# First modulations in three steps, and the first block's FFN1 as one stretch of 64-row products

## The chip, the cores and the metric

One core of a Trainium2 chip runs the whole program. The metric is the device time of one execution in microseconds (us), the median of several runs. The engines are PE (TensorE, matrix products and transposes), DVE (VectorE), ACT (ScalarE), POOL (GpSimd) and SP (SyncE, which here only issues DMAs). A product of PE reads a stationary operand that was loaded before (LDWEIGHTS, shown as PEld) and streams the other through it; it writes to PSUM, from which DVE or ACT take the result.

## What is computed

A transformer block whose normalised inputs and branches are modulated by a vector c. x is 2048 tokens by 576, all data are bf16.

```python
mod = (silu(c) @ w_mod).reshape(1, 6, 1, 576)
sa, ca, ga, sb, cb, gb = mod[:, 0] ... mod[:, 5]
h = layernorm(x) * (1 + ca) + sa
x = x + ga * attention(h)          # wqkv, feature maps, wo
h = layernorm(x) * (1 + cb) + sb
x = x + gb * (relu(h @ w1) @ w2)   # 576 -> 4608 -> 576
```

The attention is linear: 32 heads of 18, each q and k goes through a matrix w_phi of its head, and the feature map is softmax(p) beside softmax(-p).

```python
phi_q = concat([softmax(pq), softmax(-pq)]); phi_k = likewise
kv = einsum('bhsf,bhsd->bhfd', phi_k, v);  z = phi_k summed over tokens
o  = einsum('bhqf,bhfd->bhqd', phi_q, kv) / (einsum('bhqf,bhf->bhq', phi_q, z) + 1e-6)
```

## The kernel before

The 2048 tokens are 16 tiles of 128, and for the second half eight blocks of two tiles. 576 features are five chunks of rows: four of 128 and one of 64, "the half chunk" (chunk 4).

**Start.** w_mod's first 1152 columns (sa and ca, "the first modulations") are loaded into wma: one DMA for chunks 0 to 3 and one for the half chunk (load_first_mods, step LH; load_rows). first_mods(r), step MC1.r, multiplies silu(c) with them: 25 products of one column each, r = 1 the scale (ca) and r = 0 the shift (sa). first_scale (MSC) adds 1 to the scale and puts it in SBUF; first_shift (MSH) casts the shift. wqkv's columns, folded with w_phi on the chip, are multiplied by the scale into wv_sb and wfold (fold_scale, steps SCv and SC1), and the shift gives a bias row (fold_bias, steps Bv and B1, tile ps_bias). PT transposes the first normalised tiles on PE (psT_h). After that every projection (steps K, V, Q; ps_k, ps_v, ps_q) can run.

**Attention.** For each pair of tiles the feature maps take a maximum by a tree of halvings (MN, qMN), two subtractions (HI, LO; qHI, qLO) on DVE, exps on ACT (EX, qEX), row sums on DVE or PE (SU, qSD), a logarithm and an exp on ACT that give the reciprocal (RC, qRC) and a scaling on DVE (SC, qSC). Steps with a q belong to the queries of later tiles. qT transposes the map of a pair of tiles by DMA into ET. The sums kv over all tokens stand in ps_kv (KVa to KVc) and are copied with a mask into KVZ (KVE, line 640 on ACT or 642 on DVE). Then NU, NV multiply ET with KVZ (ps_num, ps_nun; NU for tiles 0 and 1, NV for 2 and 3), NUE and NVE divide (rq, o_tm), OT and OU transpose the result into oT, WO and WP multiply by wo (wo_mm for the first tiles of block 1; ps_wo), WOE and WPE add to the residual x_sb. The aux pool that holds ps_wo has two buffers, one tile of ps_wo for each half of the 576 columns; the pool of ps_h has three.

**FFN.** Per block and q = 0 to 8, FFN1 makes 4 × 128 rows of the hidden layer for 256 tokens in one PSUM tile ps_h, RL.q applies relu on ACT into H; FFN2 (step Y, ffn2_step, tile ps_y) reads H and w_sb. A step Y.j.h.p is a third (p) of the products of tile j and column half h, so it needs the relus of q = 3p to 3p + 2. In the first block FFN1 is written with G.g and FW.q: f1_whole is 16 products of 128 rows per q, f1_pairs 4 products of 64 rows per q for the half chunk, one for each half of the output partitions' set e; three q share one run of half-chunk products. In blocks 1 to 3 and after them FFN1 and wo are written in 64-row products throughout (f1_rows, wo_rows, row_halves): phase 0 multiplies rows 0 to 63 into output half e = 0 and rows 64 to 127 into e = 1, in turn, phase 1 the other way. Phase 1 must not begin in a bank before phase 0 has ended there, so a POOL memset (tile token, line 838) waits for phase 0's last product and phase 1's first product waits for it. ffn1_rows puts phase 0 of the next q between the two.

```python
for hh in range(2):
    for ci in ((4, 0, 1, 2, 3) if phase == 0 else (0, 1, 2, 3)):
        for r in range(2):
            s, e = slice(r * 64, r * 64 + 64), r ^ phase
            items.append((f1[q][:, e, hh * w:hh * w + w], l, hT[s, ci, :]))
```

**What sets the order.** Up to the end of the first block's FFN2 the program order is one string, order, at lines 1021 to 1044: names of steps (explained in the dictionary above it), in which each step issues its instructions in turn; an engine executes its own in that order. Blocks 1 to 7 are in block(n): tables say behind which product group a piece of another block's work is issued. A DMA of SP or ACT takes one of eight semaphores in turn and waits for the DMA eight before it. SP's weight loads are steps LW (w1a, w1b, w1c) and W2 (w_sb); RD.1 loads row_gb. PN transposes tiles 0 and 1 after the second norm (psT_n) and PNE modulates them into hT2all, which FFN1 reads; MCE2 adds 1 to the second scale.

Of the kernel before, what the change touches and what calls it, by code (L numbers as in the profile page):

```python
# [8 lines left out]
P = 128  # L9
# [34 lines left out]
def kernel(  # L44
# [115 lines left out]
    def load_first_mods():  # L160
        load_rows(nc.sync, wma, w_mod, 0, 2 * D)
# [44 lines left out]

# [100 lines left out]
    def first_mods(r):  # L307

        mod_ps[1, r] = aux_tile("ps_mod")
        for ci in range(KC):  # L310
            for ck in range(KC):
                o = (ck * 2 + r) * D + ci * P
                T_.matmul(mod_ps[1, r][:, ci:ci + 1], lhsT=wma_[:, o:o + P], rhs=siluc[:, ck, :],
                          start=(ck == 0), stop=(ck == KC - 1))
# [400 lines left out]
    def wo_pair(n, j):  # L715

        onum["wo", n, j] = [aux_tile("ps_wo") for _ in HALVES]
        for i, (p, (cs, cn)) in enumerate(zip(onum["wo", n, j], HALVES)):
            r = slice(i * 64, i * 64 + 64)
            T_.matmul(p[:, 0:cn], lhsT=oTs[n, j][r, 4, :], rhs=wo_sb[r, 4, cs:cs + cn], start=True, stop=False)  # L720

    def wo_mm(n, j):
        ps = onum.get(("wo", n, j))
        if ps is None:
            ps = onum["wo", n, j] = [aux_tile("ps_wo") for _ in HALVES]
            proj(ps, oTs[n, j], wo_sb, HALVES)
        else:
            for p, (cs, cn) in zip(ps, HALVES):
                for ci in range(4):
                    T_.matmul(p[:, 0:cn], lhsT=oTs[n, j][:, ci, :], rhs=wo_sb[:, ci, cs:cs + cn], start=False, stop=(ci == 3))  # L730
# [81 lines left out]
    def f1_pairs(n, q, first):  # L812
        hT, w = hT2[n], U * P
        for hh in range(2):
            for e in range(2):
                r = slice(e * 64, e * 64 + 64)
                T_.matmul(f1[q][:, e, hh * w:hh * w + w], lhsT=w1["c"][r, 2 * q + hh, :], rhs=hT[r, 4, :],  # L817
                          start=(first and hh == 0), stop=(not first and hh == 1))

    def f1_whole(n, q, first):  # L820
        hT, w = hT2[n], U * P
        for ci in range(4):
            for hh in range(2):
                for e in range(2):
                    T_.matmul(f1[q][:, e, hh * w:hh * w + w], lhsT=w1_at(2 * q + hh, e, ci),  # L825
                              rhs=hT[:, ci, :], start=(first and hh == 0 and ci == 0),
                              stop=(not first and hh == 1 and ci == 3))
# [92 lines left out]
    def ffn1(n, qs, behind={}):  # L920

        f1_open(n, qs)
        for i, q in enumerate(qs):
            f1_whole(n, q, i == 0)
            if i == 0:
                first = behind.get((q, "pairs"))
                if first:
                    first()
                for k, p in enumerate(qs):
                    f1_pairs(n, p, k > 0)  # L930
                if (q, "half") in behind:
                    behind[q, "half"]()
            f1_relu(q)
            if q in behind:
                behind[q]()

    def f1_group(g):
        qs = (3 * g, 3 * g + 1, 3 * g + 2)
        f1_open(0, qs)
        f1_whole(0, qs[0], True)  # L940
        for k, p in enumerate(qs):
            f1_pairs(0, p, k > 0)
# [28 lines left out]
    def y(n, j, cols=HALVES):  # L971
# [59 lines left out]
    QE.1 LT.11 Q.7 KE.8.1 MX.1 EX.0 QE.7 LS.15 Q.0 LX.6 Q.3 LO.3 QE.0 RS.7 SU.0 K.10 LT.9 QE.3.1 HI.3 K.11 K.9 EX.1
    KE.11 LO.2 WOL qMN.0 SA.0 LX.7 KE.10 KE.9 LT.12 SU.1 HI.2 EX.3 K.12 RW.1 RW.0 MN.2 SA.1 qMX.0 KE.12 LT.15 SU.3
    RWE.0.1 LT.14 K.15 RC.0 W1 qLO.0 K.14 RWE.1.1 LO.4 EX.2 KE.15 qHI.0 LT.13 Q.14 LO.5 MX.2 SA.3 KE.14 qEX.0 QE.14
    K.13 V.9 RC.1 HI.5 SU.2 HI.4 RC2.0 KE.13 MN.3 Q.4 LW.1.1 LO.7 VE.9 qEX.1 SA.2 V.8 EX.4 EX.5 QE.4.1 Q.13 MX.3 V.6
    VE.8 LO.6 SC.0 qSU.0 V.13 RC.2 SC.2 VE.6 qSA.0 RD.2 QE.13 Q.12 SU.5 RC.3 HI.6 VE.13 SC.3 qRC.0 V.10 EX.6 SU.4 VE.10
    SA.5 RC2.2 V.11 RC.5 QE.12 VE.11 qSC.0 V.12 SA.4 HI.7 EX.7 SC.1 SD.12 Q.8 V.15 RD.0 SD.13 SC.5 VE.12 VE.15 SU.7
    RC.4 SA.7 SC.4 RC.6 V.14 qT.0 QE.8 KVa LW.1.0 SC.6 VE.14 RC.7 KVb RC2.1 SC.7 LW.0.0 KVc Q.11 WS.1 KVE.0 KVE.1.1
    LW.0.1 QE.11 NU.1 Q.6 NU.0 LW.2.0 WS.0 NUE.1 OT.1 QE.6 Q.10 NUE.0 OT.0 OTE.1 WO.1 OTE.0 qMN.1 QE.10.1 WOE.1 WO.0
    Q.5 S2.1.1 Q.9 WOE.0 Q.15 R2.1 S2.0 R2.0 X2.1 qLO.1 X2.0 PN.1 P2 MCE2 QE.9 PN.0 QE.5.1 W2.1.1 LW.3.1 W2.0.0 PNE
# [137 lines left out]
```

## Time and profile before

| | us |
|---|---|
| median of 3 runs | 410.82 |
| the three runs | 410.12 to 411.81 |
| the profiled execution, own time | 410.89 |
| its span, first to last instruction | 409.1 |
| PE busy | 401.2 |
| DVE busy | 232.7 |
| ACT busy | 181.3 |
| granted TensorE clock | 1.000 |

The profile comes from one execution. Its span lies 1.8 us under that execution's time. PE's time is the busy time of its instructions, DVE's and ACT's likewise; a share near 100% says that the engine is the bound unless its instructions are themselves slow. The chain that ended last is followed back from the last instruction to the first: each row of it is a stretch in which that one thing held up the end, with start, length, engine, tile, line and the number of instructions. The timeline names in square brackets the idle time before an instruction and what ended it. In the table of DMA issues the last number is the median time from issue to landing.

The whole of the first block's FFN1 stands between 101.71 and 120.19 us, its FFN2 ends at 140.99, and block 1's FFN1 begins there.

### The profile page before, as it was taken

Reading aid. Unit: us, or ns where it says so; the run is one execution under the profiler, and the core shown is the slowest. Engines: PE = TensorE matmul, PEld = TensorE weight load, DVE = VectorE, ACT = ScalarE, POOL = GpSimd, SP = SyncE. Lnnn points to the kernel's source line nnn. Section 1 sums busy time; section 2 is a strip of 40 time slices with the busy share of each in tenths; the row PEclk is TensorE's granted clock in tenths of the full one; section 3 lists DMA queues with packets and bytes.
Section 4 is the critical chain, followed back from the end, with each engine's and each line's share of the span. In section 5 each row is a group of like instructions: output and inputs, shape, how many; then the busy total and the mean of one; then the engine's idle time right before and its main releaser. Section 6 shows DMA issues by size and latency. Waiting matters only on the chain.

```text
span 409.1 us, 10340 instructions
## 1 busy us (share of the span) xinstructions
PE 401.2 (98%) x4416; PEld 299.3 (73%) x4416; DVE 232.7 (57%) x600; ACT 181.3 (44%) x339; POOL 18.2 (4%) x112
## 2 busy tenths in 40 slices
PE   6999999999999999999999999999999999999997
PEld 3777777787887888888888888654467774447776
DVE  5889999999838586976886579523202310000121
ACT  5799999945761065216421460144530005552000
POOL 8100000000000000000000000000000000000000
DMA  8967950499861541424273216500040000000000
GB/s 254 281 102 200 217 126 18 73 248 375 272 159 32 118 48 23 101 48 72 54 99 80 42 34 86 112 2 2 2 66 14 16 23 8 2 2 0 16 16 29
DMA packets 70983, 35.50 MB, mean 87 GB/s; under 512 B 56657, under 2 KB 67418, under 8 KB 70938
## 3 DMA queue, kind: packets, MB, share of 16 engines
q1 hardware_dynamic: 70336, 34.83, 36.9%
q8 instruction: 34, 0.56, 0.6%
q10 hardware_dynamic: 602, 0.02, 0.1%
q14 instruction: 11, 0.09, 0.1%
HBM read 19.27 MB, written 2.37 MB: 53 GB/s over the span
## 4 chain that ended last, share of the span: by engine, by line
PE 95%; DMA 3%; DVE 0%; ACT 0%; SPq 0%; issue 0%
PE ps_y L957 35%; PE ps_h L834 30%; PE ps_v L449 5%; PE ps_k L449 5%; PE ps_q L449 5%; PE ps_h L825 4%; PE ps_wo L834 3%; PE ps_sum L515 2%; DMA wma<-in_w_mod_dram 2%; PE ps_kv L628 1%; PE ps_wo L449 1%; DMA kv_raw<-in_A_wqkv_dram 1%; PE ps_num L669 1%; PE ps_h L817 1%; PE ps_bias L366 1%; PE ps_fold L345 0%
## 5 line engine op out<-in xcount | busy, mean ns | idle before, releaser
L957 PE MATMUL ps_y<-w_sb,H 128*128 128x288 bf16 x864 | 109.0, 286 | 0.0
L957 PEld LDWEIGHTS <-H 128*128 128x128 bf16 x864 | 83.2, 98 | 22.0 <-issue 1.5
L965 DVE TENSOR_TENSOR outt<-ps_y,row_gb 128x288 bf16<-128x288 f32 (+2 forms) x33 | 14.7, 446 | 101.3 <-PE ps_y L957 101.3
L834 PE MATMUL ps_h<-hT2all,w1a 64*128 64x256 bf16 (+1 forms) x800 | 68.6, 312 | 0.0
L890 ACT ACTIVATE H<-ps_h 128x512 bf16<-128x512 f32 x36 | 21.5, 596 | 81.3 <-PE ps_h L834 81.3
L449 PEld LDWEIGHTS <-hT 128*128 128x128 bf16 x480 | 45.9, 97 | 12.6 <-issue 0.5
L834 PE MATMUL ps_h<-hT2all,w1b 64*128 64x256 bf16 (+1 forms) x640 | 54.9, 312 | 0.0
L834 PEld LDWEIGHTS <-w1a 64*128 64x128 bf16 x800 | 38.9, 94 | 21.1
L917 ACT ACTIVATE H<-ps_h 128x1024 bf16<-128x1024 f32 x36 | 36.1, 1018 | 35.3 <-PE ps_h L834 31.8
L834 PEld LDWEIGHTS <-w1b 64*128 64x128 bf16 x640 | 31.2, 94 | 17.3
L735 DVE TENSOR_TENSOR x_sb<-x_sb,ps_wo 128x288 bf16<-128x288 bf16 x28 | 11.6, 450 | 38.8 <-PE ps_wo L834 37.5
L957 PE MATMUL ps_y<-w_sb,H1m 128*128 128x288 bf16 (+2 forms) x270 | 32.4, 273 | 0.0
L834 PE MATMUL ps_h<-hT2all,w1c 64*128 64x256 bf16 (+1 forms) x180 | 28.4, 313 | 0.0
L957 PEld LDWEIGHTS <-H1m 128*128 128x128 bf16 x270 | 24.5, 98 | 5.2
L508 ACT ACTIVATE room<-room 128x1188 bf16<-128x1188 bf16 x16 | 18.7, 1189 | 15.9 <-DVE room L481 15.9
L449 PE MATMUL ps_v<-wv_sb,hT 128*128 128x288 bf16 x160 | 21.6, 286 | 0.0
L449 PE MATMUL ps_q<-wfold,hT 128*128 128x270 bf16 (+1 forms) x160 | 21.4, 285 | 0.0
L449 PE MATMUL ps_k<-wfold,hT 128*128 128x270 bf16 (+1 forms) x160 | 21.4, 285 | 0.0
L838 POOL MEMSET token<- 1x2 bf16 x75 | 7.1, 94 | 314.1 <-PE ps_h L834 298.2
L226 DVE BATCH_NORM_STATS2 bst<-x_sb 128x6 f32<-128x288 bf16 x46 | 18.5, 444 | 1.1 <-DMA x_sb<-in_A_x_dram 1.1
L526 DVE TENSOR_REDUCE ln_s<-room 128x66 f32<-128x1188 bf16 x14 | 18.9, 1373 | 0.1
L891 ACT ACTIVATE H1m<-ps_h 128x512 bf16<-128x512 f32 x30 | 17.8, 592 | 0.0
(165 smaller groups left out, 476.5 us busy)
## 6 DMA issues: line engine op xcount, KB each, us to landing
w_sb<-in_B_w_dram SPq DMA_DIRECT2D x6, 864.0 KB, 7.5
out_dram<-outt SPq DMA_DIRECT2D x15, 144.0 KB, 1.8
w1b<-in_B_w_dram SPq DMA_DIRECT2D x2, 1024.0 KB, 9.6
x_sb<-in_A_x_dram SPq DMA_DIRECT2D x3, 576.0 KB, 7.3
w1a<-in_B_w_dram SPq DMA_DIRECT2D x2, 768.0 KB, 4.6
kv_raw<-in_A_wqkv_dram SPq DMA_DIRECT2D x4, 288.0 KB, 5.0
wma<-in_w_mod_dram SPq DMA_DIRECT2D x1, 1152.0 KB
wmb<-in_w_mod_dram SPq DMA_DIRECT2D x2, 576.0 KB, 4.3
```

Of the source, the lines that this page charges most:

```text
L226: V.bn_stats(out=st[:, half, :], in_=x_sb[:, t0 + j, half * 288:(half + 1) * 288])
L449: T_.matmul(ps[:, 0:cn], lhsT=lhs[:, ci, :], rhs=w[:, ci, cs:cs + cn], start=(ci == 0), stop=(ci == KC - 1))
L508: A_.activation(out=E[:, j:j + k], in_=E[:, j:j + k], func=ACT.Exp)
L526: V.tensor_reduce(out=t["l", b][:, k * 22:(k + 1) * 22].rearrange("p (g s) h -> p g s h", s=2), op=ALU.add, axis=mybir.AxisListType.X, in_ ...
L735: V.tensor_tensor(out=xs[:, cs:cs + cn], in0=xs[:, cs:cs + cn], in1=p[:, 0:cn], op=ALU.add)
L825: T_.matmul(f1[q][:, e, hh * w:hh * w + w], lhsT=w1_at(2 * q + hh, e, ci), rhs=hT[:, ci, :], start=(first and hh == 0 and ci == 0), stop=( ...
L834: i = T_.matmul(ps, lhsT=l, rhs=r, start=(phase == 0 and k < 2), stop=(phase == 1 and k >= len(items) - 2))
L890: A_.activation(out=p2t["H1"].rearrange("p (e j) n -> p e j n", e=2)[:, :, i, :], in_=f1[i][:, :, 0:U * P], func=ACT.Relu)
L891: A_.activation(out=h1_more(i), in_=f1[i][:, :, U * P:], func=ACT.Relu)
L917: A_.activation(out=p2t["H1"].rearrange("p (e j) n -> p e j n", e=2)[:, :, 2 * q:2 * q + 2], in_=f1[q][:].rearrange("p e (h n) -> p e h n" ...
L957: T_.matmul(ps[:, 0, 0:cn], lhsT=h, rhs=p2t["w2"][:, k, c], start=(k == 0), stop=(k == NJ - 1))
L965: V.tensor_tensor(out=o[:, c], in0=ps[:, 0, 0:cn], in1=rows["gb"][:, c], op=ALU.mult)
```

## The change

Three things are edited, and a new order string goes with them.

1. load_first_mods brings the half chunk (64 rows, 144 KB) first, then chunks 0 and 1 and chunks 2 and 3, 576 KB each, in place of chunks 0 to 3 in one load and the half chunk last. first_mods runs in three steps: MC1.0 takes chunks 4, 0 and 1 of scale and shift without one product, 29 in all; MC1.1 the 11 that the scale still lacks; MC1.2 the 10 of the shift. The transposes PT.0 now stand between MC1.0 and MC1.1.
2. The first block's FFN1 goes through f1_rows (steps HA.q and HB.q for the two phases) and wo of tiles 2 and 3 through wo_rows (WA, WB). wo_pair, wo_mm, f1_pairs, f1_whole, ffn1 and f1_group are removed. The attention steps of tiles 4 and 5 (NW, NWE, OW, as att(2, 0) and att(2, 1) before) move from block 1's FFN1 into the first block's FFN2; block 1's table is rewritten accordingly.
3. The order string is new where this needs it, and around 88 to 102 us: KVE.1 on DVE instead of ACT, MCE2 earlier, the copies QE.10 and QE.5 on ACT, Q.5 behind PN and PNE, qHI.2 and qLO.2 behind the first NVE.0, the weight loads in another order.

```diff
     def load_first_mods():
-        load_rows(nc.sync, wma, w_mod, 0, 2 * D)
+        nc.sync.dma_start(wma[0:64, 4, :], w_mod[512:576, 0:2 * D])
+        for k in (0, 2):
+            nc.sync.dma_start(wma[:, k:k + 2, :], w_mod[k * P:(k + 2) * P, 0:2 * D].rearrange("(k p) n -> p k n", p=P))
...
     def first_mods(r):
-        mod_ps[1, r] = aux_tile("ps_mod")
-        for ci in range(KC):
-            for ck in range(KC):
-                o = (ck * 2 + r) * D + ci * P
-                T_.matmul(mod_ps[1, r][:, ci:ci + 1], lhsT=wma_[:, o:o + P], rhs=siluc[:, ck, :],
-                          start=(ck == 0), stop=(ck == KC - 1))
+        if not r:
+            mod_ps[1, 1], mod_ps[1, 0] = aux_tile("ps_mod"), aux_tile("ps_mod")
+        late = [(1, 1, KC - 1)] + [(1, ck, ci) for ck in (2, 3) for ci in range(KC)]
+        if r == 0:
+            todo = [(s, ck, ci) for s in (1, 0) for ck in (4, 0, 1) for ci in range(KC) if (s, ck, ci) not in late]
+        else:
+            todo = late if r == 1 else [(0, ck, ci) for ck in (2, 3) for ci in range(KC)]
+        for s, ck, ci in todo:
+            o = (ck * 2 + s) * D + ci * P
+            T_.matmul(mod_ps[1, s][:, ci:ci + 1], lhsT=wma_[:, o:o + P], rhs=siluc[:, ck, :],
+                      start=(ck == 4 and ci == 0), stop=(ck == 3 and ci == KC - 1))
...
-        "P2": open_p2, "G": f1_group, "FW": lambda q: f1_whole(0, q, False), "RL": f1_relu,
+        "P2": open_p2, "HA": lambda q: f1_rows(0, q, 0), "HB": lambda q: f1_rows(0, q, 1), "RL": f1_relu,
...
+        "NW": lambda j: num(2, j), "NWE": lambda j: quotient(2, j), "OW": lambda j: o_T(2, j),
-        "WP": lambda j: wo_mm(1, j), "WPE": lambda j: wo_out(1, j), "S3": lambda j: ln3[1](j),
+        "WA": lambda j: wo_rows(1, j, 0), "WB": lambda j: wo_rows(1, j, 1), "WPE": lambda j: wo_out(1, j), "S3": lambda j: ln3[1](j),
...
-    qMX.1 QE.15 qHI.1 qMX.2 G.0 LW.3.0 qMN.2 qLO.2 qEX.2 LW.2.1 FW.2 qEX.3 FW.1 RL.2 W2.1.0 RD.1 qHI.2 RL.0 RL.1 qSD.3
-    G.1 W2.0.1 RL.3 qSD.2 FW.4 qRC.1 W2.2.0 qSC.1 RL.4 FW.5 qT.1 RL.5 G.2 qEX.5 FW.8 FW.7 NV.0 NVE.0 RL.8 qEX.4 RL.7
+    HA.0 HA.1 HA.2 qMN.2 HB.0 LW.2.0 P2 HB.1 qSD.3 qEX.2 HB.2 qSD.2 LW.3.1 qMX.2 LW.3.0 W2.0.0 W2.1.0 RL.0 W2.0.1 HA.3
+    RL.1 qRC.1 RL.2 RD.1 HA.4 HB.3 HB.4 HA.5 RL.3 HA.6 W2.2.1 HB.5 RL.5 qSC.1 HB.6 W2.1.1 qT.1 NV.0 RL.6 Y.1.0.0 NVE.0
+    W2.2.0 OU.0 NV.1 qHI.2 RL.4 Y.1.0.1 HA.7 qLO.2 NVE.1 qEX.4 qSD.4 qEX.5 HA.8 OU.1 WA.0 HB.7 WB.0 qSD.5 WPE.0 qRC.2
+    HB.8 RL.7 WA.1 Y.1.1.0 qSC.2 WB.1 Y.1.1.1 WPE.1 RL.8 Y.1.0.2 S3.0 S3.1 Y.0.0.0 R3 X3 Y.1.1.2 YE.1.0 qT.2 NW.0 XT
...
         if n == 1:
-            F(3, "low")()
-            F(3, "high")()
-            ffn1_rows(n, {("b", 0): [att(2, 0)], ("b", 2): [att(2, 1), F(3, "exps", 0)], ("b", 3): [F(3, "exps", 1)],
...
-            normed(2)()
-            turned(2)()
+            ffn1_rows(n, {("a", 0): [F(3, "low"), F(3, "high")], ("b", 1): [early(2, 0)], ("b", 2): [late(2, 0), F(3, "exps", 0)],
+                          ("b", 3): [F(3, "exps", 1)], ("b", 4): [early(2, 1), F(3, "sums", 0)],
+                          ("b", 5): [late(2, 1), F(3, "sums", 1), normed(2), turned(2)], ("b", 6): [F(3, "recip", 0)],
+                          ("b", 7): [F(3, "scale", 0), turn(3)]})
```

Three places show how the instructions move. SP issues the FFN's weight loads just ahead of the transposes ET of tiles 2 and 3 (row_gb is the row of the second gate). Before:

```order
L767 DMA w1c<-in_B_w_dram 64x2304 x2
L772 DMA w1a<-in_B_w_dram 128x4x512
L778 DMA w_sb<-in_B_w_dram 128x6x576
L774 DMA w1b<-in_B_w_dram 128x4x1024
L778 DMA w_sb<-in_B_w_dram 128x6x576
L774 DMA w1b<-in_B_w_dram 128x4x1024
L772 DMA w1a<-in_B_w_dram 128x4x512
L778 DMA w_sb<-in_B_w_dram 128x6x576
L410 DMA row_gb<-four_d 128x576
L778 DMA w_sb<-in_B_w_dram 128x6x576 x2
L656 DMA_TRANSPOSE ET<-room 128x11x128 x2
L778 DMA w_sb<-in_B_w_dram 128x6x576
```

and with the change:

```order
L757 DMA w1c<-in_B_w_dram 64x2304
L762 DMA w1a<-in_B_w_dram 128x4x512
L757 DMA w1c<-in_B_w_dram 64x2304
L762 DMA w1a<-in_B_w_dram 128x4x512
L764 DMA w1b<-in_B_w_dram 128x4x1024 x2
L768 DMA w_sb<-in_B_w_dram 128x6x576 x3
L416 DMA row_gb<-four_d 128x576
L768 DMA w_sb<-in_B_w_dram 128x6x576 x2
L662 DMA_TRANSPOSE ET<-room 128x11x128 x2
L768 DMA w_sb<-in_B_w_dram 128x6x576
```

The same loads stand ahead of ET, w1 now ahead of w_sb. ACT in the first block's FFN1, from the second norm's modulation to the second reciprocal (H<-ps_h is a relu, room<-room 128x11x108 an exp, ln_s and rsum the reciprocal). Before:

```order
L419 ACTIVATE hT2all<-psT_n,mod_171 128x256 x2
L88 ACTIVATE room<-ps_q 128x540
L88 ACTIVATE room<-ps_q 128x18x2
L508 ACTIVATE room<-room 128x11x108 x2
L917 ACTIVATE H_1822<-ps_h 128x2x512 x4
L531 ACTIVATE ln_s<-ln_s 128x132
L533 ACTIVATE rsum<-ln_s 128x264
L917 ACTIVATE H_1822<-ps_h 128x2x512 x2
L508 ACTIVATE room<-room 128x11x108
L917 ACTIVATE H_1822<-ps_h 128x2x512
L508 ACTIVATE room<-room 128x11x108
L917 ACTIVATE H_1822<-ps_h 128x2x512 x2
```

and with the change:

```order
L514 ACTIVATE room<-room 128x11x108 x2
L891 ACTIVATE H_1937<-ps_h 128x2x512 x2
L537 ACTIVATE ln_s<-ln_s 128x132
L539 ACTIVATE rsum<-ln_s 128x264
L891 ACTIVATE H_1937<-ps_h 128x2x512 x5
L514 ACTIVATE room<-room 128x11x108 x2
L537 ACTIVATE ln_s<-ln_s 128x132
L539 ACTIVATE rsum<-ln_s 128x264
L891 ACTIVATE H_1937<-ps_h 128x2x512 x2
```

The first reciprocal stands behind two relus instead of four; the last two relus now stand behind the second reciprocal. DVE from the query maximum of pair 1 (tree, root) to the modulation for FFN1 (hT2all). Before:

```order
L471 TENSOR_TENSOR root<-tree 128x132
L90 CAST room<-ps_q 128x540
L90 CAST room<-ps_q 128x18x2
L713 TENSOR_TENSOR x_sb<-x_sb,ps_wo 128x576 x2
L226 BN_STATS bst<-x_sb 128x6 x2
L227 BN_AGGR mv<-bst 128x2
L238 TENSOR_SCALAR xn<-x_sb,mv,rstd 128x576
L479 TENSOR_TENSOR room<-root,pq_173 128x22x54
L238 TENSOR_SCALAR xn<-x_sb,mv,rstd 128x576
L327 TENSOR_SCALAR mod_171<-mod_171 128x5
L90 CAST room<-ps_q 128x540
L90 CAST room<-ps_q 128x18x2
L420 TENSOR_SCALAR hT2all<-psT_n,mod_171 128x256 x3
```

and with the change:

```order
L477 TENSOR_TENSOR root<-tree 128x132
L333 TENSOR_SCALAR mod_171<-mod_171 128x5
L719 TENSOR_TENSOR x_sb<-x_sb,ps_wo 128x576 x2
L227 BN_STATS bst<-x_sb 128x6 x2
L228 BN_AGGR mv<-bst 128x2
L239 TENSOR_SCALAR xn<-x_sb,mv,rstd 128x576 x2
L485 TENSOR_TENSOR room<-root,pq_173 128x22x54
L426 TENSOR_SCALAR hT2all<-psT_n,mod_171 128x256 x3
```

Four casts of projections leave DVE here, the addition to the second scale goes ahead of the residual, and the subtraction for pair 1 goes behind both normalised tiles.

More of the change, by code (lines that the diff above doesn't have):

```diff
@@ L713, in res_first @@
         V.tensor_tensor(out=xs, in0=xs, in1=onum["wo", j][:, :, 0:288], op=ALU.add)
[L715 to L730, printed above, removed]
     def wo_out(n, j):
@@ L810, in f1_open @@
             f1[q] = mm_tile("ps_h")
[L812 to L827, printed above, removed]
     last = {}
@@ L918, in f1_relu @@
                       in_=f1[q][:].rearrange("p e (h n) -> p e h n", h=2), func=ACT.Relu)
[L920 to L942, printed above, removed]
     f2 = {}
@@ L1031 @@
[L1031 to L1039, printed above, removed]
-    qMX.1 QE.15 qHI.1 qMX.2 G.0 LW.3.0 qMN.2 qLO.2 qEX.2 LW.2.1 FW.2 qEX.3 FW.1 RL.2 W2.1.0 RD.1 qHI.2 RL.0 RL.1 qSD.3
```

31 lines of the change are left out of this document (18 added, 13 removed).

## The prediction

> **What bounds the kernel now.** I read the page first: busy time by engine, and the shares of the chain that ended last.
>
> ```profile
> PE 401.2 (98%) x4416; PEld 299.3 (73%) x4416; DVE 232.7 (57%) x600; ACT 181.3 (44%) x339; POOL 18.2 (4%) x112
> PE 95%; DMA 3%; DVE 0%; ACT 0%; SPq 0%; issue 0%
> ```
>
> TensorE (PE) is busy 401.2 of 409.1 us and is 95% of the chain. A change can gain only where PE stands idle, or by making PE's own work shorter. The table by stretches says where it is idle; its columns are stretch, length, busy time of PE, PEld, DVE, ACT and POOL, clock, DMA share and GB/s.
>
> ```profile
> 0.00:20.00 20.00, 15.59 (x178) 11.39 (x179) 14.20 (x51) 12.81 (x31) 9.44 (x32) 1.00 1.06 273
> ...
> 88.00:102.00 14.00, 13.52 (x149) 10.61 (x146) 12.12 (x34) 7.67 (x23) 0.00 (x0) 1.00 1.03 344
> 102.00:141.00 39.00, 39.00 (x367) 31.67 (x367) 25.01 (x61) 15.97 (x22) 0.00 (x0) 1.00 0.56 146
> ```
>
> PE lacks 4.4 us in the first 20, 0.5 us between 88 and 102, and nothing from 102 to 141. The granted clock is 1.00 in all three. So the change has two small holes to fill, and otherwise must shorten a full stream.
>
> **The start.** The chain of waits has, in order of time (start, length, what):
>
> ```profile
> 6.60 8.22 DMA wma<-in_w_mod_dram
> 14.87 0.68 PE ps_mod L313 x21
> 15.54 0.58 PE psT_h L262 x10
> 16.12 0.62 PE ps_mod L313 x25
> 16.77 0.16 DVE room L321
> 17.00 1.38 PE ps_bias L366 x20
> ```
>
> The last 144 KB of wma are issued at 6.60 and land at 14.82; the 21 products behind them then run at 0.62/25 = 25 ns each, ten transposes, 25 products of the shift, a cast, and the bias product at 17.00. DVE in the same place:
>
> ```profile
> 15.58 0.17 DVE L318 TENSOR_SCALAR mod<-ps_mod 128x5 f32<-128x5 f32 x1 [0.24 <-PE ps_mod L313]
> 15.78 0.65 DVE L358 TENSOR_SCALAR wv_sb<-kv_raw,mod 128x576 bf16<-128x576 bf16 x2
> 16.77 0.16 DVE L321 CAST room<-ps_mod 128x4 bf16<-128x4 f32 x1 [0.33 <-PE ps_mod L313]
> ```
>
> After the change 29 products run on the half chunk and chunks 0 and 1, behind PT.1's end at 14.12 (14.87 less the four products that ran ahead, 0.25, and the wait of 0.50): until 14.12 + 29 × 0.025 = 14.85. The ten transposes (0.58) end at 15.43. Only then is the last load needed, which with the same bytes ahead of it lands near 14.82: 0.6 us to spare, so the wait of 0.50 us goes. Eleven products end the scale at about 15.85, 0.3 later than now; ten more (0.25) end the shift at 16.1. DVE takes the scale (0.17) and two wv_sb (0.65) from 15.90, and casts from 16.7, against 16.77 now. PE loses its wait, but the casts then wait for DVE, which has no slack. **Term a: −0.1**, from −0.4 (the casts go ahead of the second wv_sb's end) to +0.3 (the later scale is passed on whole).
>
> **The head of FFN1.** Chain rows between the attention's sums and the first FFN1 product:
>
> ```profile
> 88.58 0.64 DVE KVZ L642
> 89.44 0.81 ACT KVZ L640 x4
> 90.29 0.18 PE ps_num L669
> 90.47 1.23 PE ps_q L449 x10
> ...
> 101.15 0.42 DVE hT2all L420
> 101.58 0.14 issue
> 101.71 1.91 PE ps_h L825 x16
> ```
>
> ACT's second part of KVZ (ready at 90.25, held up behind DVE's 0.64) becomes two small DVE copies, a third of the width together; behind 88.58 + 0.64 they are ready near 89.6, some 0.6 earlier. PE gains little there, 0.1 to 0.2, because a Q projection covers most of the wait. At the end, PNE's modulation (0.42, and 0.14 of issue) is now covered by projection Q.5, which moved behind PN.0: its ten products (1.23, as in the row above) are longer than the 0.56. Against that, Q.5 no longer covers a quotient earlier: 0.1. **Term b: −0.15 − 0.56 + 0.1 = −0.6**, from −0.8 (with no such loss) to 0 (if the quotients take the whole gain).
>
> **FFN1's rows.** Before, nine q of 16 whole products and 4 half ones:
>
> ```profile
> 103.62 0.76 PE ps_h L817 x12
> 104.38 5.35 PE ps_h L825 x48
> 120.19 0.23 PE ps_num L669 x8
> 126.78 1.23 PE ps_wo L449 x10
> 185.54 0.61 PE ps_wo L834 x10
> 186.15 1.96 PE ps_h L834 x36
> 188.11 0.49 PE ps_wo L834 x8
> 188.60 3.93 PE ps_h L834 x72
> ```
>
> That stage took 120.19 − 101.71 = 18.48 us, with 5.35/48 = 111.5 ns for a whole product. A later block, already written in 64-row products, shows 1.96/36 = 54.4 ns and 3.93/72 = 54.6 ns for one half: two take 109 ns. After: 9 × 36 = 324 products × 54.5 = 17.66. Entering this form from whole products costs something: 12 halves took 0.76 where 12 × 54.5 = 0.65, so 0.11 an entry, three entries (start, after NV.0 and its FFN2 step, after the next FFN2 step): 0.33. Sum 17.99. **Term c: −0.5**, from −0.83 (no entry cost) to 0.
>
> The Trainium skill, "TensorEngine Tiling (Array Packing)", Key Properties, says that changing the tiling mode drains the TensorE. The 0.76 against 0.65 agrees with that. By the same page's Overview, splitting rows helps where the contraction is at most 64, and here it is 512 plus 64; by that rule term c would be near zero, which is the third rival below.
>
> Wo of tiles 2 and 3: 1.23 each becomes 0.61 + 0.49 = 1.10. **Term d: −0.26.** Two num steps of tiles 4 and 5 (0.31 to 0.34 with 0.08) move from block 1 to the first block's FFN2: nothing gained or lost on a full PE.
>
> **The new waits.** HA and HB of one q need a POOL memset between them, and the code puts another q's products there (1.96 us of cover), as blocks 1 to 3 already do without a gap. What PE has not had so far is NV.0, WA.1 and the FFN2 steps this early. Durations for the walk:
>
> ```profile
> 112.55 1.47 DVE L543 TENSOR_TENSOR room<-room,rsum 128x1188 bf16<-128x1188 bf16 x2 [0.83 <-ACT rsum L533]
> 120.46 0.18 DVE L677 TENSOR_SCALAR rq<-ps_num 128x24 f32<-128x24 f32 x1 [6.45 <-PE ps_num L669]
> 122.00 0.18 DVE L684 COPY o_tm<-o_tm 128x64 bf16<-128x64 bf16 x1
> 122.09 1.38 DVE L526 TENSOR_REDUCE ln_s<-room 128x66 f32<-128x1188 bf16 x1
> 104.54 2.28 ACT L508 ACTIVATE room<-room 128x1188 bf16<-128x1188 bf16 x2 [1.52 <-DVE room L481]
> L735 DVE TENSOR_TENSOR x_sb<-x_sb,ps_wo 128x288 bf16<-128x288 bf16 x28 | 11.6, 450 | 38.8 <-PE ps_wo L834 37.5
> 107.65 0.78 DVE L479 TENSOR_TENSOR room<-root,room 128x1188 bf16<-128x1188 bf16 x1
> ```
>
> From NV.0's end to WPE.0's end DVE and ACT have: quotient and copy 1.72 (120.46 to 122.18), the two exponent inputs 1.55, the first exp 1.14, two sums of 1.38, two residual adds of 0.45: 8.1 us, and up to 1.02 more where a relu stands ahead of the exps. PE has two FFN2 steps (1.48 each), 0.31 for NV.1, and HA.7, HA.8, HB.7, HB.8, WA.0 and WB.0 in between: 2 × 1.48 + 0.31 + 2 × 1.96 + 1.10 = 8.3. WA.1 needs the two PSUM tiles that WPE.0 frees, so it waits 0 to 0.8: I take 0.27, nearer the low end, because that relu can run while ACT still waits for the exponents' inputs. The same delay sits in front of RL.7, queued on ACT behind qRC.2; the FFN2 step that reads its H waits 0.28 (0 to 0.5). Two shorter ones, HA.3 for a PSUM tile that RL.0 frees behind an exp, and NV.1 for the quotient (1.5 against a step of 1.48), come to 0.18 (0 to 0.3). **Term e: +0.73**, from 0 to 1.6.
>
> NV.0 also needs the transposed feature maps (ET) of tiles 2 and 3. Their scale ended at 112.55 + 1.47 = 114.02; now DVE does one max tree instead of two and one exponent input instead of two ahead of the sums, which brings it to about 111.0.
>
> ```profile
> 114.16 3.14 SPq L656 DMA_TRANSPOSE ET<-room  x2
> ET<-room SPq DMA_TRANSPOSE x16, 3.7
> row_ga<-four_d SPq DMA_DIRECT2D x1, 144.0 KB, 3.2
> row_gb<-four_d SPq DMA_DIRECT2D x1, 144.0 KB, 11.5
> ```
>
> Issued at 111.1, landed 3.7 later at 114.8. PE reaches NV.0 at 101.1 + 7 × 1.96 + 0.2 = 115.0. It is hidden by only 0.2 us: any later landing is a wait of PE, one for one. I take 0 for it.
>
> **Sum:** −0.1 − 0.6 − 0.5 − 0.26 + 0.73 = −0.73. Against the profiled run's own 410.89 that is 410.16; that run is 0.07 above the median of 410.82, so the forecast is 410.1. With every term at its own bounds, taken as independent, it goes from about 409.2 to 411.0. A measurement of this kernel can tell about 0.5%, which is 2.05 us, from no change: below 408.77 is faster, above 412.87 slower.
>
> **The rivals.**
> 1. *The gains come unspoiled.* No new wait, each gain at its low end: −0.4 − 0.8 − 0.83 − 0.26 = −2.29, so 408.5. For it: the 8.1 us chain is shorter than PE's 8.3 as long as no relu stands ahead. Against: four separate slacks, each within 0.3 us, must all hold.
> 2. *ET lands late, and it is slower.* The loads of w1b and w_sb now all stand before ET on SP with few steps between; row_gb, of the same size and kind as row_ga, took 11.5 against 3.2, so 8.3 us can go in standing behind such loads. If ET's transposes meet half of it, 4.15, less the 0.2 of slack, PE waits 3.95: 414.0. It decides from a landing after 117.8 (2.8 us late). Against it: the present kernel's ET transposes of these tiles also stand behind all of these loads but one, and 3.7 is the median of all sixteen. The Trainium skill, "DMA: Bandwidth & Descriptors", Queues, rings and completion order, gives the ground: each (row, engine) pair is one ring, and what an issuing engine sends stands there in order. The two rows for row_ga and row_gb agree.
> 3. *Halves do not pay in the first block.* Two halves take as long as one whole product: 162 × 111.5 ns = 18.06, and with the entries 18.39, which leaves −0.1 of term c; wo likewise loses its 0.26. 410.1 + 0.4 + 0.26 = 410.8. For it: weights load 128 rows at once in the whole form and twice 64 in the other. Against: the row of 72 in 3.93 is the same shape.
> 4. *The three steps do not fill the start.* The last two chunks land after 15.43 as one load of 576 KB, on queues that are at 1.06 of their share: 0.5 to 1 us late gives 410.6 to 411.1. Against: the bytes are the same, and the half chunk no longer comes last.
>
> **How the numbers follow.** Forecast 0.47 (own range 409.2 to 411.0), rival 1 0.23, rival 2 0.12, rival 3 0.10, rival 4 0.08. Faster by over 0.5%: four fifths of rival 1 and a twentieth of the rest of the low side, 0.22. Slower: nearly all of rival 2, with a little for a mishap in the forecast, 0.13. Within: 0.65. The range must leave out at most 0.2: from 408.3 it takes in about two thirds of rival 1, the forecast, rivals 3 and 4, and ends at 411.9: 0.8.
>
> **What would show it.** In the changed profile: (a) no wait of PE for wma, the casts within 0.3 of 16.77, ps_bias at about 16.9; (b) the first ps_h product at 101.1, with no wait for hT2all ahead of it; (c) rows of 36 products at 1.96 in the first block; the stage from the first ps_h to the last, less the other steps between, at 18.0; (d) ps_wo of 0.61 and 0.49 before 141; (e) PE's waits between 102 and 141 in all below 1.6, on WPE and relu results and not on ET; ET's landing at 3.7. The prediction is wrong if a wait for ET above 1 us stands there, if the products of the first block take over 55 ns, or if the time before 88 moves by more than 0.4.

## The result, and the profile after

| | before | changed |
|---|---|---|
| median, us (16 runs each) | 410.60 | 409.63 |
| lowest and highest | 409.34, 413.14 | 408.15, 410.32 |
| span of the profiled execution | 409.1 | 407.7 |

The ratio of the changed kernel to the one before is 0.9969, with a 95% interval from 0.9955 to 0.9982: faster by 0.7 to 1.8 us, less than the 2.05 us named as clear of no change. The forecast was 410.1. The page and the table by stretches of the changed kernel, with the columns as before:

```profile
PE 400.4 (98%) x4576; PEld 299.4 (73%) x4576; DVE 231.3 (57%) x598; ACT 181.3 (44%) x338; POOL 19.4 (5%) x123
0.00:20.00 20.00, 15.69 (x181) 11.54 (x182) 14.59 (x51) 12.99 (x31) 9.53 (x33) 1.00 0.98 275
88.00:102.00 14.00, 13.96 (x156) 10.74 (x153) 12.11 (x37) 8.59 (x23) 0.00 (x0) 1.00 1.06 342
102.00:141.00 39.00, 39.00 (x540) 31.74 (x538) 27.32 (x71) 15.31 (x21) 0.98 (x11) 1.00 0.64 157
```

PE's hole between 88 and 102 is closed (13.96 of 14), the one in the first 20 us is not (15.69 against 15.59). The chain of waits at the start (start, length, what), and PE's wait in the table of waits:

```profile
13.39 0.57 PE psT_h L263 x10
13.96 0.70 PE ps_mod L319 x29
14.67 0.58 PE psT_h L263 x10
15.25 0.27 PE ps_mod L319 x11
15.74 0.84 DVE wv_sb L364 x2
16.58 0.07 DVE room L327
16.72 1.37 PE ps_bias L372 x20
PE ps_bias L372 <- DVE room L328: 0.6, 1, 0.6
```

The wait for wma is gone, and a wait of 0.57 for DVE's casts stands in its place. From the first psT_h's start to the bias product it is 3.46 us in the timeline (13.24 to 16.70) and was 3.47 before (13.51 to 16.98). That the bias product comes 0.28 earlier is due to what lies ahead of it: the 18 transposes that wait for kv_raw (ps_wT) start 0.07 earlier and take 0.19 less. When kv_raw lands differs from execution to execution. The chain through the first block:

```profile
100.98 13.86 PE ps_h L808 x252
114.84 0.34 PE ps_num L675 x8
115.25 1.48 PE ps_y L908 x12
118.60 2.29 PE ps_h L808 x40
121.50 0.87 PE ps_h L808 x16
122.87 0.87 PE ps_h L808 x16
123.74 0.81 PE ps_wo L808 x10
124.55 1.58 PE ps_y L908 x12
126.13 0.60 PE ps_wo L808 x8
132.71 0.23 PE ps_num L675 x8
140.69 5.13 PE ps_h L808 x92
160.69 8.93 PE ps_y L908 x72
```

FFN1 starts 84.26 us behind the bias product's start (84.71 before): the head gives 0.45. From the first FFN1 product to block 1's FFN2 it is 59.71 us (100.98 to 160.69), and was 60.32 (101.71 to 162.03): 0.61 less. Of this, the first block takes 39.71 against 39.28, with the two moved num steps, 0.62, now in it; block 1's FFN1 takes 20.00 against 21.04, 1.04 less, though only 0.62 of work left it.

### The profile page after: what moved, and what is told of

Same layout as the page of the kernel before. It is cut to its first block, busy times and chain, and to the rows that moved or that the text cites. A ratio compares the mean times of both kernels' runs of the same rounds, so it can differ in the third digit from the quotient of the medians.

```text
span 407.7 us, 10677 instructions
## 1 busy us (share of the span) xinstructions
PE 400.4 (98%) x4576; PEld 299.4 (73%) x4576; DVE 231.3 (57%) x598; ACT 181.3 (44%) x338; POOL 19.4 (5%) x123
## 4 chain that ended last, share of the span: by engine, by line
PE 97%; DMA 1%; DVE 0%; ACT 0%; SPq 0%; issue 0%
PE ps_y L908 35%; PE ps_h L808 35%; PE ps_v L455 5%; PE ps_q L455 5%; PE ps_k L455 5%; PE ps_wo L808 4%; PE ps_sum L521 2%; PE ps_kv L634 1%; DMA kv_raw<-in_A_wqkv_dram 1%; PE ps_num L675 1%; PE ps_wT L341 1%; PE ps_fold L351 1%; PE ps_wo L455 1%; PE ps_bias L372 1%; PE ps_row L387 0%; ACT room L88 0%
## 5 line engine op out<-in xcount | busy, mean ns | idle before, releaser
L808 PE MATMUL ps_h<-hT2all,w1a 64*128 64x256 bf16 (+1 forms) x960 | 78.5, 305 | 0.0
L808 PEld LDWEIGHTS <-w1a 64*128 64x128 bf16 x960 | 47.0, 94 | 21.8
L808 PE MATMUL ps_h<-hT2all,w1b 64*128 64x256 bf16 (+1 forms) x768 | 62.8, 305 | 0.0
L808 PEld LDWEIGHTS <-w1b 64*128 64x128 bf16 x768 | 37.6, 94 | 17.9
L808 PE MATMUL ps_h<-hT2all,w1c 64*128 64x256 bf16 (+1 forms) x216 | 33.4, 306 | 0.0
L514 ACT ACTIVATE room<-room 128x1188 bf16<-128x1188 bf16 x16 | 18.7, 1189 | 15.0 <-DVE room L487 13.5
L812 POOL MEMSET token<- 1x2 bf16 x86 | 8.2, 96 | 311.9 <-PE ps_h L808 291.7
```

The lines of the kernel that those rows point to most:

```text
L514: A_.activation(out=E[:, j:j + k], in_=E[:, j:j + k], func=ACT.Exp)
L808: i = T_.matmul(ps, lhsT=l, rhs=r, start=(phase == 0 and k < 2), stop=(phase == 1 and k >= len(items) - 2))
L812: g = last[key] = G.memset(token[:], 0.0)
```

## The experiments

**Undoing the start.**

```diff
-PT.1 MC1.0 ... FA1.3 PT.0 MC1.1 ... MSC MC1.2 SCv.1 SCv.0 MSH      (loads: half chunk, 0-1, 2-3)
+PT.1 ... FA1.3 MC1.1 ... MSC PT.0 SCv.1 MC1.0 SCv.0 MSH            (loads: chunks 0-3, half chunk)
```

The step of load_first_mods in the string is LA. LH loads the matrices w_phi; the change had also put it at the head of the string, and this edit puts it back behind LA.

> The changed kernel with the loads and products of the first modulations as before (four chunks, then the half chunk; scale and shift as 25 products each; PT.0 behind the scale). Theory: the three steps are worth what the two profiles differ by at the first bias product, 17.00 against 16.72, so this one starts the bias product at 17.0 and its whole span is 0.3 longer than the changed kernel's 407.7 (408.0). Rival: the start is hidden later (the first K and V projections wait for something else as well), then the bias product is late but the first FFN1 product stands at 100.98 as in the changed kernel. Other rival: the new start also changes when DMA semaphores come round and so more than 0.3 hangs on it: 0.6 or more.

Measured: ratio to before 0.9976 (0.9957 to 0.9995), span 406.8, shorter than the changed kernel's. The timeline of PE:

```profile
12.45 0.72 PE L261 MATMUL psT_h<-ident,xn 128*128 128x128 bf16 x10
13.64 0.68 PE L312 MATMUL ps_mod<-siluc,wma 128*128 128x1 bf16 x21 [0.39 <-DMA wma<-in_w_mod_dram]
15.75 0.78 PE L365 MATMUL ps_bias<-kv_raw,room 128*1 128x288 bf16 x10
```

Neither the theory nor its rivals hold: from psT_h to the bias product it is 3.30 here, 0.16 less than with the three steps, and the rest of the kernel is as in the changed one. In this execution kv_raw and wma came early: the last load of wma landed at 13.59, and at 14.82 in the kernel before. One profile doesn't price the start, and the times don't either: the medians are 409.37 and, for the changed kernel, 409.63, and the intervals of the two ratios overlap.

**The start alone**, in the kernel before: the same edit the other way.

> The kernel before with the new start alone (loads, three steps, PT.0 moved), all the rest as before. Theory: the first bias product moves from 17.00 to 16.7 and everything behind it by 0.3: span 408.8 against 409.1, first FFN1 product at 101.4. Rival: other parts of the change are needed for it (the head waits for KVZ or loads anyway): first FFN1 product at 101.7, span unchanged.

Measured: 0.9975 (0.9959 to 0.9991), median 409.99 against 410.49. Span 408.2; the bias product stands at 16.18, and from there to the end it is 392.0 against 392.1. So the profile shows no gain behind the bias product and 3.45 from psT_h to it, and yet the median falls by half a microsecond, and the ratio says a whole one. The list of all executions tells most of why. Of 92 executions of the kernel before, 24 had a mean granted clock of 0.995 or 0.996, and those took 411.35 to 412.31; the others, at 0.999 or 1.000, took 409.09 to 410.90. With the new start it was 2 of 100 executions of ten kernels, none of this kernel's 12; with the old start in the changed kernel 4 of 12, at 410.60 to 411.04 against 408.43 to 409.75 for the rest.

At the full clock the two pairs disagree. In the kernel before, the new start is 0.28 faster (medians 409.99 and 410.27, run side by side). In the changed kernel the old start's eight such executions have a median of 408.94, and the changed kernel's 16, not run beside them, 409.63. The profiles suggest why an early load can favour the old start: in all nine with the new start and no wait for wma, psT_h to the bias product takes 3.41 to 3.46, with 0.51 to 0.57 of it spent on the casts; the old start's 3.47 and 3.30 hold waits for wma of 0.50 and 0.39, and without them would be 2.9 to 3.0, by estimate.

**A later load, in both.** To see where that clock comes from, one load of x was put ahead of the first modulations' loads.

```diff
-... LA ... LP4.2 ...
+... LP4.2 LA ...
```

> The kernel before with a load of x (576 KB, two later pairs of tiles) moved ahead of the first modulations' loads. Theory: with the old start the last wma load sets the chain, so its lateness goes through: at some 275 GB/s the load takes 2.1 us, PE's wait for wma grows from 0.5 to about 2.6 and the time by 2. Rival: the loads run side by side on many queues and wma's landing moves by much less, below 0.7.

> The changed kernel with the same load of x moved ahead of the first modulations' loads. Theory: the new start has about 1 us of slack before the last pair of chunks is needed, so of 2.1 us about 1 goes through: PE waits about 1 for wma and the time grows by 0.5 to 1, at least 0.7 less than with the old start. This would say why the kernels with the new start gain in their medians what one pair of profiles doesn't show. Rival: the new order of loads has no more slack than the old one: the same growth in both.

Measured: with the old start 1.0060 (1.0040 to 1.0079), median 413.08, and 8 of 10 executions at a clock of 0.991 to 0.996; with the new start 1.0003 (0.9987 to 1.0019), median 410.35, 3 of 10. Waits of PE, old and then new, with the old one's table by stretches below (the column before the last two is the granted clock):

```profile
PE ps_mod L313 <- DMA wma<-in_w_mod_dram: 1.8, 2, 1.1
...
13.50:14.00 0.50, 0.29 (x6) 0.12 (x3) 0.23 (x2) 0.10 (x1) 0.00 (x0) 1.00 0.98 263
14.00:14.50 0.50, 0.00 (x0) 0.00 (x0) 0.50 (x2) 0.08 (x1) 0.00 (x0) 1.00 1.19 272
14.50:15.00 0.50, 0.11 (x4) 0.11 (x4) 0.40 (x1) 0.50 (x2) 0.00 (x0) 1.00 0.97 175
15.00:15.50 0.50, 0.15 (x4) 0.06 (x3) 0.00 (x0) 0.23 (x2) 0.00 (x0) 1.00 0.81 223
17.50:18.00 0.50, 0.48 (x11) 0.18 (x9) 0.27 (x3) 0.50 (x2) 0.25 (x2) 0.85 1.01 305
19.00:20.00 1.00, 1.00 (x12) 0.52 (x8) 0.96 (x4) 0.58 (x2) 0.55 (x5) 0.50 2.90 286
21.00:21.50 0.50, 0.50 (x5) 0.35 (x4) 0.50 (x3) 0.46 (x3) 0.00 (x0) 0.73 0.64 136
21.50:22.00 0.50, 0.50 (x6) 0.40 (x5) 0.50 (x2) 0.36 (x1) 0.28 (x1) 1.00 3.11 171
```

```profile
PE ps_mod L319 <- DMA wma<-in_w_mod_dram: 0.4, 2, 0.3
```

With the old start PE is idle for most of 13.8 to 15.8, and two microseconds later its clock is at half speed, from 17.9 to 21.3. The ten bias products take 1.36 instead of 0.78 in the timeline. The new start lets 0.4 of waiting through where the old one has 1.8, and its clock stays at 1.00 in this execution. So the three steps buy a margin against a late load, and not an unlimited one, as the 3 of 10 say. Against their own kernels the times grew by some 0.6% and 0.34%, 2.5 and 1.4 us. The size fits: 3.4 us at half speed lose 1.7 us, which is 0.4% of the span, so the mean clock is 0.996. The 24 executions of the kernel before at 0.995 or 0.996 are 1.7 longer than the others (medians 411.89 and 410.21). None of them was traced; that their clock comes from the same wait is argued from this pair, the size and the counts.

**The num steps back in block 1**, with block 1's table as before.

```diff
-Y.1.1.2 YE.1.0 qT.2 NW.0 XT NWE.0 Y.0.1.0 ... NW.1 OW.0 ... NWE.1 ... OW.1 ...
+Y.1.1.2 YE.1.0 qT.2 XT Y.0.1.0 ...
-            ffn1_rows(n, {("a", 0): [F(3, "low"), F(3, "high")], ("b", 1): [early(2, 0)], ...
+            F(3, "low")(); F(3, "high")()
+            ffn1_rows(n, {("b", 0): [att(2, 0)], ("b", 2): [att(2, 1), F(3, "exps", 0)], ...
```

> The changed kernel with the num, quotient and transposes of tiles 4 and 5 back in block 1, and block 1's table as before. Theory: each num step that stands between 64-row products costs two changes of form on top of its own 0.31, about 0.11 each, so two steps cost 0.44 more there than among whole products: block 1's FFN1 takes 21.0 us again instead of 20.0, the first block's FFN2 becomes 0.62 shorter, and the whole is 0.4 slower than the changed kernel. Rival (the prediction's own assumption): the steps only move, nothing gained or lost: within 0.1 of the changed kernel's span.

Measured: 0.9982 (0.9967 to 0.9998), span 409.0. The interval overlaps the changed kernel's, so the price is read from the chain:

```profile
143.97 0.34 PE ps_num L675 x8
144.38 4.04 PE ps_h L808 x72
```

Block 1's FFN1 takes 140.80 to 161.84, 21.04, as expected: a num step costs 0.34 here where it costs 0.23 among whole products, and the 72 products behind it 4.04 where they else take 3.93. The two steps together are 0.42 dearer here. Of the 1.3 by which the spans differ, another 0.63 is a wait for ET at NV.0, which this edit didn't touch.

**Whole products per q.**

```diff
-"HA": lambda q: f1_rows(0, q, 0), "HB": lambda q: f1_rows(0, q, 1),
+"HA": lambda q: (f1_open(0, (q,)), f1_pairs(0, q, True)), "HB": lambda q: f1_whole(0, q, False),
```

f1_pairs and f1_whole are those of the kernel before, and a q's relus and places in the order stay.

> The changed kernel with the first block's FFN1 in the same order, but per q the four 64-row products of the half chunk and then 16 whole products of 128 rows, so a change of form twice per q (no wait of POOL any more). Theory: a whole product takes 0.111, a half one 0.0545, a change of form 0.11: per q 1.79 + 0.22 + 0.22 = 2.23 against 1.97 now, nine times 0.26 = 2.4 us slower than the changed kernel, a span near 410. Rival that a change of form costs nothing and the 0.11 was a pipeline effect of the two banks: per q 2.01, 0.4 slower. Rival that halves do not pay: no slower than the changed kernel.

Measured: 1.0027 (1.0005 to 1.0049), span 409.7. The chain:

```profile
102.28 5.35 PE ps_h L816 x48
107.63 0.54 PE ps_h L808 x8
108.17 3.60 PE ps_h L816 x32
121.52 1.85 PE ps_h L816 x16
```

Runs of 48, 32 and 16 whole products differ by 1.75 for 16, that is 0.1094 each, and every run has 0.10 on top. Eight halves take 0.54, 0.44 by the 0.0545 each and 0.10 on top. So two halves (0.109) cost what one whole product costs, and a change of form costs 0.10 to 0.11 in each direction. The size of the loss came near the expectation, but partly for another reason: the order puts HA.0 to HA.2 and others together, so there are fewer than 18 changes, and 0.7 of waits for the projections' copies and 0.5 for oT came instead.

**Waits, first try: an FFN2 step ahead of WA.1.**

```diff
-WB.0 qSD.5 WPE.0 qRC.2 HB.8 RL.7 WA.1 Y.1.1.0 qSC.2 WB.1
+WB.0 qSD.5 WPE.0 qRC.2 Y.1.1.0 HB.8 RL.7 WA.1 qSC.2 WB.1
```

> The changed kernel with the FFN2 step Y.1.1.0 moved ahead of HB.8 and WA.1, which then stand together with WB.1. Theory: WA.1's wait of 0.20 for the PSUM tiles that WPE.0 frees is covered by the step's 1.48, and the number of changes of form stays the same: 0.2 faster than the changed kernel, FFN2 of the first block ending near 140.5. Rival: the relu of q 8 comes 1.5 us later and the step that reads it then waits, up to 0.5: no gain or slower.

Measured: 1.0015 (0.9998 to 1.0032), slower than the changed kernel. Its table of waits has

```profile
PE ps_y L908 <- ACT H L891: 1.4, 1, 1.4
PE ps_wo L808 <- POOL token L812: 0.3, 1, 0.3
```

The step opens a fourth tile in a pool of three (q 7, q 8 and the other tile of Y hold them), so it waits 1.4 for the relu that frees one. Neither theory nor rival had seen that. And without a step between them WB.1 waits 0.3 for the memset between its phases.

**The head, in two parts:** KVE.1 on ACT again, and Q.5 ahead of PN instead of behind PNE.

```diff
-... KVE.0 LW.2.1 KVE.1 ...
+... KVE.0 LW.2.1 KVE.1.1 ...
```

> The changed kernel with the second part of KVZ copied by ACT again, in five operations. Theory: NU.1's sums then wait for KVZ again; of the ACT copy's 0.8 behind DVE's 0.64 a projection of 1.23 covers most, so 0.1 to 0.4 slower up to the first FFN1 product (101.1 to 101.4 instead of 100.98). Rival: nothing, since Q.11 covers it whole: 100.98.

```diff
-... Q.15 X2.1 X2.0 Q.9 qLO.1 PN.1 PN.0 QE.15 PNE Q.5 QE.5 ...
+... Q.15 Q.5 X2.1 X2.0 Q.9 qLO.1 PN.1 PN.0 QE.15 PNE QE.5 ...
```

> The changed kernel with projection Q.5 ahead of the transposes PN instead of behind PNE, so that nothing covers PNE's modulation. Theory: FFN1's first product waits 0.4 to 0.6 for hT2all, as before: it starts at 101.4 to 101.6 instead of 100.98. Rival: PN itself waits for the normalised tiles now and Q.5 ahead of it covers that, so that the wait only moves: 100.98 to 101.1.

Measured: 0.9969 (0.9951 to 0.9988) and 0.9986 (0.9968 to 1.0004), which the intervals don't separate from the changed kernel; what follows is read from one profile each. Timelines, first of the one and then of the other:

```profile
89.42 0.86 PE L675 MATMUL ps_num<-KVZ,ET 108*128 108x57 bf16 x11
101.38 0.28 PE L808 MATMUL ps_h<-hT2all,w1c 64*128 64x256 bf16 x2
```

```profile
101.25 0.29 PE L808 MATMUL ps_h<-hT2all,w1c 64*128 64x256 bf16 x2 [1.11 <-ACT hT2all L425]
```

With ACT's copy the eleven num products stretch to 0.86 (0.47 with DVE's), and from the sums over the tokens to FFN1 it is 0.37 longer than in the changed kernel (18.16 against 17.79 in the chains): the upper end of what was expected. Without its cover FFN1 waits 1.11 for hT2all and the same stretch is 0.9 longer, more than the 0.4 to 0.6 expected.

**Loads ahead of ET:** one load of w_sb more, and one less.

```diff
-... HB.6 W2.1.1 qT.1 NV.0 RL.6 Y.1.0.0 NVE.0 W2.2.0 OU.0 ...
+... HB.6 W2.1.1 W2.2.0 qT.1 NV.0 RL.6 Y.1.0.0 NVE.0 OU.0 ...
```

> The changed kernel with one more load of w_sb (864 KB) ahead of the transposes ET of tiles 2 and 3. Rival 2 of the prediction says that transposes stand behind such loads: at 350 GB/s 864 KB are 2.5 us, the queue that ran dry near 110 runs on to 112 and ET, issued at 110, lands up to 2.5 later, so NV.0 waits 1 to 2 us for it. Theory: the loads that are issued by 103 are done by then and ET's landing stays at 3.6 to 3.9: no wait above 0.4.

```diff
-... RL.3 HA.6 W2.2.1 HB.5 ... HA.8 OU.1 WA.0 ...
+... RL.3 HA.6 HB.5 ... HA.8 OU.1 W2.2.1 WA.0 ...
```

> The changed kernel with one load of w_sb less (864 KB, the last third's second half) ahead of the transposes ET of tiles 2 and 3; it is issued behind the transposes of o instead. Theory: one load more made NV.0 wait 1.6 and five profiles of the changed order show waits of 0 to 0.6, so one load less lets ET land within 4 us and NV.0 waits for nothing: products from the first ps_h to NV.0 in 13.8, and the time 0.1 to 0.6 under the changed kernel's. Rival: the load now lands late for the third FFN2 step (issued near 121.5, needed near 128), which then waits 1 or more.

Measured: 410.46 in the one execution of the first, which is too few for a time, and 0.9971 for the second (0.9957 to 0.9985). SP's issue of the two transposes and PE's first num product, with one load more and then with one less:

```profile
109.37 5.30 SPq L662 DMA_TRANSPOSE ET<-room  x2
115.78 0.41 PE L675 MATMUL ps_num<-KVZ,ET 108*128 108x57 bf16 x8 [1.64 <-DMA ET<-room]
```

```profile
109.48 4.01 SPq L662 DMA_TRANSPOSE ET<-room  x2
114.18 0.41 PE L675 MATMUL ps_num<-KVZ,ET 108*128 108x57 bf16 x8
```

One load more costs 1.64 of waiting, as the second rival of the prediction would have it. One load less gains nothing: the DMA engines are nearly idle from 108 on (13 GB/s, then none), and SP still needs 4.0 for the two, more than in the changed kernel (3.75) and in the kernel before (3.14). Other profiles of the same order show 4.0 to 4.5, and in five of them PE waits 0.3 to 0.6 for ET. So the loads ahead don't stretch the issue of the two transposes, up to one more. What does is not settled, but the 14 traces divide cleanly. In the ten kernels with FFN1 in 64-row products the issue takes 3.75 to 5.30, and one packet of the queue that loads instructions (q8) runs during it. In the four with whole products it takes 3.13 or 3.14 with no such packet; one of them is the whole products per q above, with this order and the same loads ahead. The DMA packets of each queue during the issue (packets, MB, share of 16 engines), of that kernel (109.57 to 112.70) and then of the changed one (110.07 to 113.82):

```profile
q1 hardware_dynamic: 1565, 0.43, 69.8%
```

```profile
q1 hardware_dynamic: 1357, 0.40, 83.4%
q8 instruction: 1, 0.02, 1.9%
```

The 64-row kernels have more instructions to load (10,677 in the changed one, 10,340 before; 36 packets of q8 against 34). That the load is what holds up the transposes is argued: no run moved it.

**Casts first.** With one load less, and the casts of the shift ahead of the scaled rows:

```diff
-MSC MC1.2 SCv.1 SCv.0 MSH
+MSC MC1.2 MSH SCv.1 SCv.0
```

> As the run with one load less, and with the casts of the shift on DVE ahead of the two wv_sb rows of the scale. In every profile of the new start ps_bias waits 0.51 to 0.57 for these casts. Theory: the casts end 0.6 to 0.7 earlier, ps_bias has no wait, and as the V products behind it find their scaled weights in time the whole gains 0.3 to 0.5 on the run with one load less (first bias product 2.9 us behind the first transpose psT_h instead of 3.45). Rival: the wait moves to the first V product, which needs the wv_sb rows that are now later by 0.2: 0 to 0.2 gained.

Measured: 0.9952 (0.9936 to 0.9968), median 408.85 in 6 runs (408.03 to 409.08): below both kernels, though its interval overlaps that of the changed one. The timeline:

```profile
12.43 0.72 PE L263 MATMUL psT_h<-ident,xn 128*128 128x128 bf16 x10
15.24 0.78 PE L372 MATMUL ps_bias<-kv_raw,room 128*1 128x288 bf16 x10
113.91 0.41 PE L675 MATMUL ps_num<-KVZ,ET 108*128 108x57 bf16 x8 [0.51 <-DMA ET<-room]
```

From psT_h to the bias product it is 2.81 instead of 3.45, with no wait there, and the 30 V products behind it take 3.78 as before: the theory, with 0.64 above its upper end of 0.5. The wait for ET is back at 0.51, with the load removed.

## Why the prediction was right, and where its steps were not

The time lay in the range and moved the way that was forecast; the gain was 1.0 (medians) to 1.3 us (ratio) where 0.73 was forecast. That it came so near is in part luck. A share of the gain, 0.4 if 24 of 92 executions of the kernel before lose 1.7 each, is the half-speed stretch, of which the prediction knew nothing. In the pair of profiles the terms as they came out are 0 for a (−0.1 forecast), −0.45 for b (−0.6), −0.59 for c (−0.5), −0.26 for d (as forecast), +0.65 for e (+0.73) and −0.42 for the moved num steps (0): −1.07 in all. Two of these, c and e, have the right size for the wrong reason.

- **Term a, −0.1.** The mechanism came as worked out: no wait for wma, a scale ready at 15.54, casts behind two wv_sb rows, and next to nothing gained (3.46 against 3.47). One sum is off by 0.14: eleven products behind 15.43 end at 15.71, not 15.85. What the term left out is how the load's landing varies. At the full clock the sign of what the new start changes stays open (−0.28 in one pair, +0.69 in the other). Over many executions it also avoids a half-speed stretch, which about a quarter of those of the kernel before seem to have had, at some 1.7 us each.
- **Term b, −0.6.** The sum was 0.45, its parts were mis-sized in both directions. KVZ by DVE is worth 0.37 (0.15 forecast): the projection covers less of the wait than assumed. Covering PNE is worth more than forecast if taken away (0.9), but against the kernel before there remains 0.1 of the 0.56, since PN.0 now waits for the second normalised tile (DVE ends it at 99.02 and PN.0 starts at 99.07): the two steps' transposes stretch from 98.55 to 99.65, 1.10, and took 0.69 before.
- **Term c, −0.5.** Right in size and wrong in its reason. FFN1's products take 13.86 + 2.29 + 0.87 + 0.87 = 17.89 (17.99 forecast). But the step "111.5 ns for a whole product" divided a run that contains a change of form: a whole product costs 109.4, the same as two halves, so the form by itself gains 324 × 0.0545 = 17.66 against 144 × 0.1094 + 36 × 0.0545 = 17.71, which is 0.05. What the term gained is fewer changes of form in FFN1: of the 18.48 before, 0.77 was changes, of the 17.89 now 0.23. The third rival was right that the halves don't pay, and wrong in what follows from it. The Trainium skill's sentence in "TensorEngine Tiling (Array Packing)", Key Properties, that changing the mode drains the array, agrees with these 0.10 to 0.11.
- **Term d, −0.26.** The products alone do that (the half chunk costs half): 0.61 + 0.49 each. But WB.1 stands behind an FFN2 step and pays 0.11 for it, and WA.1 takes 0.81 instead of 0.61, so the four rows add up to 2.51 against 2.46 before. The 0.11 and the 0.20 are counted under e.
- **"Nothing gained or lost" for the moved num steps** is the step that failed. Four changes of form around them in block 1 went away: 0.42, shown by putting them back.
- **Term e, +0.73.** In the changed kernel's profile the only new wait is WA.1's 0.20. The table of waits doesn't list it; that it is for WPE.0's tiles is read from DVE, whose two residual adds end at 123.73, just ahead of WA.1's third LDWEIGHTS at 123.78. RL.7, RL.0 and NVE.0 make nobody wait. But where NV.0, WB.1 and two FFN2 steps follow products of the other form, 0.11 + 0.11 + 0.23 = 0.45 is paid in changes of form, which the term lacked. For FFN2 it shows in the chains: before, a long row,

```profile
130.70 10.29 PE ps_y L957 x84
```

gives 0.1225 a product, while the 12 behind WA.1 take 1.58 and the 48 behind WB.1 5.99, 0.11 more than that each. ET, called hidden by only 0.2, was the tightest point indeed: it is waited for in five of the eight other profiles that have this order up to NV.0 with its loads as they are or fewer, 0.3 to 0.6 each. The second rival's wait came only with one load more.

By rows of the two chains, block 0 and block 1's FFN1 come to −0.59 (c) + 0.05 (wo) + 0.11 (NV) + 0.23 (FFN2's changes) − 0.42 (num steps) = −0.62, and 0.61 was measured.

## What to carry to other kernels

Count the changes between products of different row height along PE's order, at 0.1 us each way here, before counting products: gathering them was the gain, not the form itself, and a small step moved out of a foreign run gains twice that. Price a run of products from two runs of different length, so that what is paid once per run drops out. For a wait on a load near the start, look at the granted clock of all executions and not at one profile, since how late it can come decides more than its mean; and where such a wait goes, name the engine that is late next: here one swap on DVE was worth more than the edit that uncovered it.

## What the runs showed of the hardware

PE's granted clock fell to 0.50 for 3.4 us (17.9 to about 21.3) in one execution, two microseconds after PE had been idle for 1.45 of the 2.0 us from 13.5 to 15.5, by the windows above. The Trainium skill, "TensorE: Matmul & The Clock Gate", What's actually happening, gives half rate after an idle window of about 3.4 us and full rate again after as long a busy one. The length at half rate agrees; the idle time ahead of it was shorter here, and broken by two bursts of products. That this idle time brought it about is argued from one trace.

Changes between 64-row and 128-row products cost 0.10 to 0.11 us in both directions. SP's issue of two DMA transposes of the same size took 3.14, 4.01 and 4.48 us in three kernels with almost no load in flight ahead of them, and 5.30 with one. In all 14 traces it was above 3.2 us where a packet of the instruction queue ran during it, and only there.
